# Tile 6's second product as seven half-size products, and three weight groups a stage later

## The chip, the cores and the metric

The kernel runs on one core of a Trainium2 chip. The core has a matrix engine (PE, with its weight loads shown apart as PEld), a vector engine (DVE), a scalar engine (ACT), a general engine (POOL) and a queue engine (SP) that issues DMAs here. Each engine works through its own instructions in order. [...]

The metric is the time of one execution on the device in microseconds, the median of several runs.

## What is computed

Attention with a sliding window of 64 keys over 8 batches of 8 heads, 576 positions and head size 64, and then a layer with a cosine gate over the 4608 x 512 result:

```python
scores = scale * np.matmul(q, k.transpose(0, 1, 3, 2))
rel = pos[:, None] - pos[None, :]
mask = (rel >= 0) & (rel < window)            # window = 64
attn = softmax(np.where(mask, scores, -1e9))
x = np.matmul(attn, v)                        # as (4608, 512)
h = x @ w_in                                  # (4608, 2048)
g = h * np.cos(h)
out = g @ w_out                               # (4608, 512)
```

## The kernel before

The 4608 rows are cut into nine tiles of 512 rows (mt = 0 to 8). For tiles 1 to 8 a stage has 32 units of planned time (T = 32, the first half Q = 16). In the first half PE computes h for the tile, 16 blocks of 128 columns with four matmuls each (`first`, L479). For each block ACT takes the sine (L709) and DVE multiplies (the gate, L712) into a tile gT. The h blocks go round five PSUM banks named O1, X0, X1, S and O0 (`H_BANKS`), so a bank is free for the fifth block after it once the gate has read it. In the second half PE multiplies the gates with w_out: 64 matmuls of 512 columns into banks O1 and O0, 16 per block of 128 rows, each block copied out by DVE or ACT (L723 to L727).

In tiles 7 and 8 (`FAST`) the second half is a Strassen-Winograd scheme (`fast_second`): the 512 x 2048 by 2048 x 512 product is cut into 2 x 2 blocks and done as seven products P1 to P7 of 16 matmuls of 256 columns. It needs sums of blocks of w_out (T0 to T3, `sum_weights`, L499, made over earlier stages by POOL and DVE) and sums of blocks of the gates (`sum_rows`, L511, on DVE after the last gate). The products' parts are combined when they are read from PSUM: `keep` leaves p1, t6 and t56 in SBUF, `result` writes the output. T2 and T3 lie in the buffers of q and k and are made by POOL in tile 6's stage.

Attention for the batches 2 to 7 is woven into these stages. Each batch has nine groups of four units. `burst_scores` puts the scores of several groups into PSUM at once (a first burst of four groups at 14.6 units, a second of five at 20.2). For each group follow `g_max` (mask and maximum, DVE, L347), `g_exp` (exponentials with row sums, ACT, L359), `g_inv` (reciprocal, DVE, L369), `g_norm` (POOL, L376) and `g_trans` (a transposing DMA on SP's queue, L395), one group every `PACE` = 1.44 units. `values` (L411) multiplies with v, and `put_x` copies the result, on DVE or ACT, into xT, which the next tile's h reads. Batch 7 does this in tile 6's stage; its groups 0 and 1 are needed by tile 7's values, the rest by tile 8's. Values for a tile come at the end of the stage before (T x mt - 1.01), those for tile 8 earlier (- 8.01).

The order is written out by hand: `at(time, fn, ...)` puts a step into a plan, and `pump(time)`, called after each block of h and after each piece of a product, issues everything planned up to that time. The order in which steps are issued is the order on each engine. In tile 6 before, the second half pumps one unit after every four matmuls of 512 columns; in a seven-product tile it pumps 16/14 of a unit after every eight matmuls of 256 columns.

Of the kernel before, what the change touches and what calls it, by code (L numbers as in the profile page):

```python
# [40 lines left out]
FAST = (7, 8)  # L41
PRODUCTS = ("P1", "P2", "P6", "P5", "P7", "P3", "P4")
# [27 lines left out]
def kernel(  # L70
# [45 lines left out]
    H_BANKS = [banks * 3 + [last] for *banks, last in (["O1", "X0", "X1", "S", "O0", "X0"], ["X1", "S", "X0", "O1", "O0", "S"])]  # L116
# [159 lines left out]
    for b in range(2, B):  # L276
        alone = NU // 2 if b == 3 else NU - 1
        steps = [(0, 2), (2, 4)], [(alone,)] + [(5, 7), (7, 9)] if b == 3 else [(4, 6), (6, 8), (alone,)]
        for banks, starts in zip(BURSTS, steps):
# [58 lines left out]
    def g_max(n):  # L338
# [4 lines left out]
        else:  # L343
            s = att.tile([128, GF, 128], F32, tag="s", name="s", bufs=6)
# [106 lines left out]
    def gate_half(g, f):  # L451
        if ("g", f) not in st:
            st["g", f] = moe.tile([128, 2, MT], BF16, tag="gT", name="gT", bufs=n_ff // 2 + 2)
# [22 lines left out]
    def first(mt, ff, ks, start, stop):  # L476
        if start:
            st["h", ff] = bank(H_BANKS[mt == 1][ff], "h_ps")
# [10 lines left out]

    def b_block(k_, j):  # L490
        return w_out_sb[:, n_ff // 2 * k_:n_ff // 2 * k_ + n_ff // 2, half * j:half * j + half]

    def sum_weights(i, f, engine):
        d = slice(2 * f, 2 * f + 2)
        if ("T", i) not in st:
            st["T", i] = w_sums[:, i] if i < 2 else rows_tile("qk"[i - 2])[:, 0:n_ff // 2 * half].rearrange("p (a n) -> p a n", n=half)
        in0, in1 = ((b_block(0, 1), b_block(0, 0)), (b_block(1, 1), st["T", 0]),
                    (b_block(1, 1), b_block(0, 1)), (b_block(1, 0), st.get(("T", 1))))[i]
        (nc.gpsimd if engine == "p" else nc.vector).tensor_tensor(out=st["T", i][:, d], in0=in0[:, d], in1=in1[:, d], op=ALU.subtract)  # L499

    def sum_rows(gT):
        sums = [[att.tile([128, 4, half], BF16, tag="se"[i], name="sums", bufs=6) for i in range(2)] for _ in range(4)]
        s1, s2, s3, s4 = [[pair[i // 2][:, 2 * (i % 2):2 * (i % 2) + 2] for i in range(4)] for pair in sums]
        a = [[[gT[f + 4 * k_][:, :, half * i:half * i + half] for f in range(4)] for k_ in range(2)] for i in range(2)]

        def sums_now(*which):
            for i in which:
                to, in0, in1, op = ((s1, a[1][0], a[1][1], ALU.add), (s2, s1, a[0][0], ALU.subtract),
                                    (s3, a[0][0], a[1][0], ALU.subtract), (s4, a[0][1], s2, ALU.subtract))[i]
                for f in range(4):  # L510
                    nc.vector.tensor_tensor(out=to[f], in0=in0[f], in1=in1[f], op=op)  # L511
        sums_now(0, 1)
        return sums_now, {"P1": a[0][0], "P2": a[0][1], "P4": a[1][1], "P5": s1, "P6": s2, "P7": s3, "P3": s4}

    def fast_second(mt, gT):
        sums_now, lhs = sum_rows(gT)
# [13 lines left out]
        def result(o_sb, c, of, other, block=None):  # L530
            for n in range(len(blocks)) if of == apart and block is None else (block,):
                d, lo, hi = (slice(0, 2), 0, half) if n is None else blocks[n]
                cols = slice(half * c + lo, half * c + hi)
                nc.vector.tensor_tensor(out=o_sb[:, d, cols], in0=acc[of] if n is None else acc[of][n],
                                        in1=temp[other][:, d, lo:hi], op=ALU.add)
# [7 lines left out]
        def after_p2():  # L543
            result(o1, 0, "P2", "p1")
            sums_now(2)

        def after_p6():
            keep("t6", "P6", "p1")
            sums_now(3)
# [3 lines left out]
        after = {"P1": lambda: keep("p1", "P1"), "P2": after_p2, "P6": after_p6, "P5": lambda: keep("t56", "P5", "t6"),  # L553
                 "P7": lambda: result(o2, 1, "P7", "t56"), "P3": lambda: result(o1, 1, "P3", "t56"),
                 "P4": lambda: result(o2, 0, "P7", "t6")}
        for n, name in enumerate(PRODUCTS):
# [5 lines left out]
            to = acc[name if new else "P7"]  # L562
            split = type(to) is list
            for n_, (e, lo, hi) in enumerate(blocks if split else ((0, 0, half), (1, 0, half))):
                for f in range(n_ff // 2):
                    nc.tensor.matmul(out=to[n_] if split else to[:, e], lhsT=lhs[name][f // 2][:, f % 2, 128 * e:128 * e + 128],  # L566
                                     rhs=rhs[name][:, f, lo:hi], start=new and f == 0 and (e == 0 or split),
# [22 lines left out]
    for i, (b, jobs, banks) in enumerate(bursts):  # L590
        t = T * (b - 1)
        at(t + BURST[i % 2] + 0.9 * (i == 1), burst_scores, i)
# [53 lines left out]
    for n in range(16):  # L646
# [3 lines left out]
        else:  # L650
            at(T * (FAST[0] - 1) + (5.8 if i == 2 else 9.8) + f, sum_weights, i, f, "p")
# [41 lines left out]
    for mt in range(1, n_mt):  # L693
# [5 lines left out]
        for ff in range(n_ff):  # L699
# [5 lines left out]
            if ff % 2 == 0:  # L705
                gt = moe.tile([128, 2, MT], BF16, tag="gT", name="gT", bufs=n_ff // 2 + 2)
                gT.append(gt)
            e = ff % 2
            nc.scalar.activation(sin, h_ps, AF.Sin, bias=math.pi / 2.0)  # L709
            if ff == n_ff - 1 and mt < B - 1:  # L710
                exp_table()
            nc.vector.tensor_tensor(out=gt[:, e], in0=h_ps, in1=sin, op=ALU.mult)  # L712
            pump(base + ff)
# [3 lines left out]
        for ms0 in range(0, MT // 128, 2):  # L717
            o_sb = moe.tile([128, 2, d_model], F32, tag="out", name="out_sb", bufs=OUTS)
            o_ps = [bank(which, "out_ps") for which in (("O1",) if mt == n_mt - 1 and ms0 else ("O1", "O0"))]
            for e in range(2):  # L720
                ms = ms0 + e
                for ff in range(n_ff):
                    nc.tensor.matmul(out=o_ps[e], lhsT=gT[ff // 2][:, ff % 2, ms * 128:ms * 128 + 128],  # L723
# [39 lines left out]
```

## Time and profile before

| | us |
|---|---|
| median of 3 runs | 302.15 |
| lowest, highest | 302.14, 304.46 |
| span of the profiled execution | 301.0 |
| PE busy | 294.0 (98%) |
| DVE busy | 234.7 (78%) |
| ACT busy | 232.2 (77%) |
| POOL busy | 210.3 (70%) |

The span runs from the first to the last instruction of one profiled execution. The granted PE clock is full throughout. A row of a timeline or of the chain gives the start, the length, the engine, the line of the kernel, the operation with its output and input, and a count; in brackets stands how long the engine was idle before and who released it. Busy times of PE are partly modelled, since matmuls overlap, so the distance from one start to the next says more than a row's length.

### The profile page before, as it was taken

The page shows a single profiled execution, that of the slowest core. Times are in us where ns is not written, and L with a number is a line of the kernel's source. Part 1 is how long each engine was busy: PE and PEld are TensorE (multiplying, and loading weights), DVE is VectorE, ACT ScalarE, POOL GpSimd, SP SyncE. Part 2 cuts the span into 40 slices and gives each one's busy share as a digit, 9 for nine tenths or more (in the row PEclk, how much of TensorE's full clock was granted, in tenths as well). Part 3 has the DMA queues.
Part 4 walks back from the last instruction along what each step waited for, and adds up shares of the span by engine and source line. Part 5 has one row for each costly group of instructions (what it writes and reads, how often), then busy time and mean ns, then how long its engine had stood idle before and what let it go on. Part 6 is the DMA issues. An engine that isn't in the chain of part 4 may idle for free.

```text
span 301.0 us, 8375 instructions
## 1 busy us (share of the span) xinstructions
PE 294.0 (98%) x2863; PEld 162.5 (54%) x2863; DVE 234.7 (78%) x916; ACT 232.2 (77%) x781; POOL 210.3 (70%) x238
## 2 busy tenths in 40 slices
PE   8888999999999999999999999999999999999996
PEld 3667854644455445444454445444544454785485
DVE  4997888898887886788678876887588658985794
ACT  5997699877987699769986998699978997304610
POOL 8999568995899579995999599969997860000000
PEclk9999999999999999999999999999999999999999
DMA  7999999999999994999999999999999745003013
GB/s 146 179 206 195 198 186 138 99 154 156 219 124 112 230 119 75 115 152 188 174 108 145 165 216 115 126 152 205 134 101 119 212 86 174 2 3 139 1 37 105
DMA packets 159627, 41.45 MB, mean 138 GB/s; under 512 B 146976, under 2 KB 155232, under 8 KB 159584
## 3 DMA queue, kind: packets, MB, share of 16 engines
q0 software_dynamic: 101088, 18.06, 79.6%
q1 hardware_dynamic: 58352, 22.79, 42.3%
q8 instruction: 22, 0.36, 0.5%
q14 instruction: 21, 0.17, 0.2%
q10 hardware_dynamic: 144, 0.07, 0.1%
HBM read 36.70 MB, written 9.44 MB: 153 GB/s over the span
## 4 chain that ended last, share of the span: by engine, by line
PE 90%; DMA 4%; POOL 4%; DVE 1%; issue 0%; POOLq 0%
PE h_ps L479 37%; PE out_ps L723 28%; PE out_ps L566 8%; PE out_ps L462 5%; DMA w_in<-in_moe_w_in_dram 4%; PE h_ps L443 4%; PE s_ps L310 3%; PE o_ps L411 3%; PE tq_ps L223 1%; POOL v L186 1%; POOL q L164 1%; POOL k L164 1%; PE s_ps L332 1%; POOL w_in L202 0%; DVE xT L125 0%; PE tw_ps L392 0%
## 5 line engine op out<-in xcount | busy, mean ns | idle before, releaser
L479 PE MATMUL h_ps<-xT,w_in 128*128 128x512 bf16 x512 | 115.1, 379 | 0.2
L712 DVE TENSOR_TENSOR gT<-h_ps,sin 128x512 bf16<-128x512 f32 x128 | 85.2, 688 | 25.8 <-ACT sin L709 25.2
L709 ACT ACTIVATE sin<-h_ps 128x512 f32<-128x512 f32 x128 | 73.8, 598 | 37.0 <-PE h_ps L479 36.7
L359 ACT ACTIVATE e<-s,negm 128x128 f32<-128x128 f32 (+1 forms) x256 | 97.1, 382 | 1.7 <-POOL v L125 1.0
L723 PE MATMUL out_ps<-w_out,gT 128*128 128x512 bf16 x384 | 85.3, 379 | 0.0
L376 POOL TENSOR_TENSOR w<-e,rden 128x512 bf16<-128x512 f32 (+1 forms) x68 | 69.0, 1032 | 21.8 <-DVE rden L369 15.9
L479 PEld LDWEIGHTS <-w_in 128*128 128x128 bf16 x512 | 48.9, 98 | 54.5
L723 PEld LDWEIGHTS <-gT 128*128 128x128 bf16 x384 | 36.5, 98 | 43.1
L347 DVE CUSTOM_DVE_ANT_0 s<-s_ps,mask 128x128 f32<-128x128 f32 (+1 forms) x256 | 56.0, 277 | 1.8 <-PE s_ps L332 1.5
L359 ACT ACTIVATION_READ_ACCUMULATOR e<-s,negm 128x1 f32 x256 | 48.1, 188 | 0.0
L186 POOL DMA_DIRECT2D v<-in_v_dram x40 | 34.1, 870 | 0.1
L180 POOL DMA_DIRECT2D q<-in_q_dram x36 | 28.7, 801 | 7.7 <-DMA k<-in_k_dram 3.0
L180 POOL DMA_DIRECT2D k<-in_k_dram x36 | 28.7, 799 | 1.5 <-DVE gT L712 0.7
L369 DVE RECIPROCAL rden<-den 128x4 f32<-128x4 f32 (+1 forms) x73 | 12.2, 167 | 18.7 <-ACT e L359 18.3
L125 POOL COPY v<-v 64x1536 bf16<-64x1536 bf16 (+3 forms) x16 | 22.9, 1433 | 0.4
L347 DVE DVE_READ_ACCUMULATOR2_ANT negm<- 128x1 f32 x256 | 21.3, 83 | 0.0
L125 DVE CAST xT<-o_ps 128x512 bf16<-128x512 f32 x24 | 15.6, 679 | 4.6 <-PE o_ps L411 4.4
L443 PE MATMUL h_ps<-xT,w_in 128*128 128x256 bf16 x128 | 14.6, 273 | 0.4 <-DMA w_in<-in_moe_w_in_dram 0.4
L462 PE MATMUL out_ps<-w_out,gT 128*128 128x512 bf16 x64 | 14.8, 380 | 0.0
L443 PEld LDWEIGHTS <-w_in 128*128 128x128 bf16 x128 | 12.3, 98 | 2.1 <-DMA w_in<-in_moe_w_in_dram 0.7
L566 PEld LDWEIGHTS <-sums 128*128 128x128 bf16 x136 | 12.2, 98 | 2.0 <-DVE sums L511 0.4
L449 ACT ACTIVATE sin<-h_ps 128x512 f32<-128x512 f32 x16 | 9.3, 596 | 4.2 <-PE h_ps L443 4.2
(92 smaller groups left out, 309.4 us busy)
## 6 DMA issues: line engine op xcount, KB each, us to landing
out_dram<-out_sb SPq DMA_DIRECT2D x16, 512.0 KB, 8.3
v<-in_v_dram POOLq DMA_DIRECT2D x32, 128.0 KB, 5.6
q<-in_q_dram POOLq DMA_DIRECT2D x36, 96.0 KB, 7.3
k<-in_k_dram POOLq DMA_DIRECT2D x36, 96.0 KB, 6.1
w_in<-in_moe_w_in_dram POOLq DMA_DIRECT2D x4, 512.0 KB, 9.6
w_out<-in_moe_w_out_dram POOLq DMA_DIRECT2D x4, 512.0 KB, 11.0
q<-in_q_dram POOLq DMA_DIRECT2D x7, 144.0 KB, 5.6
k<-in_k_dram POOLq DMA_DIRECT2D x7, 144.0 KB, 5.7
```

Source lines behind the costliest of these rows:

```text
L125: {"a": nc.scalar.copy, "p": nc.gpsimd.tensor_copy}.get(engine, nc.vector.tensor_copy)(out, in_)
L180: nc.gpsimd.dma_start(out=st[name, b][:, c].rearrange("p (h d) -> p h d", h=H), in_=src.rearrange("h p d -> p h d"))
L186: nc.gpsimd.dma_start(out=vt.rearrange("p (h d) -> p h d", h=H), in_=v[b, :, c * 128:c * 128 + n, :].rearrange("h p d -> p h d"))
L347: nc.vector.tensor_tensor_reduce(out=s[:, u, c], in0=s_ps[:, u, c], in1=mask[:, 2 - j % 2 if j else 0, c], scale=-scale if b else -1.0, sc ...
L359: nc.scalar.activation(e[:, u, c], s[:, u, c], AF.Exp, bias=negm[:, u:u + 1], scale=1.0 if n < n_first else -1.0, accum_out=den[:, u:u + 1])
L376: (nc.gpsimd if engine == "p" else nc.vector).tensor_tensor(out=w[:, 0:u], in0=e[:, 0:u], op=ALU.mult, in1=rden[:, 0:u].unsqueeze(2).to_br ...
L443: nc.tensor.matmul(out=h_ps[:, half * e:half * e + half], lhsT=w_in_sb[:, ks, ff * 128:ff * 128 + 128], rhs=st["xT", 0][:, ks, half * g:ha ...
L479: nc.tensor.matmul(out=st["h", ff], lhsT=w_in_sb[:, ks, ff * 128:ff * 128 + 128], rhs=st["xT", mt][:, ks], start=start, stop=stop)
L566: nc.tensor.matmul(out=to[n_] if split else to[:, e], lhsT=lhs[name][f // 2][:, f % 2, 128 * e:128 * e + 128], rhs=rhs[name][:, f, lo:hi], ...
L709: nc.scalar.activation(sin, h_ps, AF.Sin, bias=math.pi / 2.0)
L712: nc.vector.tensor_tensor(out=gt[:, e], in0=h_ps, in1=sin, op=ALU.mult)
L723: nc.tensor.matmul(out=o_ps[e], lhsT=gT[ff // 2][:, ff % 2, ms * 128:ms * 128 + 128], rhs=w_out_sb[:, ff], start=ff == 0, stop=ff == n_ff - 1)
```

## The change

`FAST` becomes (6, 7, 8). The seven products use two banks instead of three, in the order P1, P6, P2, P5, P7, P3, P4: P2 is added onto P1 in its bank after ACT has copied p1 out, P5 and then P3 onto P6 after DVE has kept t6 and t56, and P4 onto P7, which takes the bank of P1 once ACT has copied P1 + P2 to the output. The two banks swap roles from tile to tile, and `H_BANKS` of tiles 7 and 8 follow.

The halves of the inner dimension are now interleaved in pairs, four gates share one gT tile, and the first two row sums are made on DVE behind every fourth gate. The third (a difference) overwrites gate blocks in place: in tile 6 on DVE after P6, in tiles 7 and 8 on POOL behind every fourth gate. The fourth is made on DVE after P2. The buffers of s go from six to four.

Batch 7's second burst has two groups left; its last three groups get a burst of their own in tile 7's stage at 14.6 units, and tile 8's values move to the usual place. ACT loads the table of the exponential in tile 7 as well.

```diff
-FAST = (7, 8)
-PRODUCTS = ("P1", "P2", "P6", "P5", "P7", "P3", "P4")
+FAST = (6, 7, 8)
+LATE = 6
+FAMILY = ("O1", "O0")
+PRODUCTS = ("P1", "P6", "P2", "P5", "P7", "P3", "P4")
...
+    H_BANKS = {mt: ["X0", "X1", FAMILY[(mt - FAST[0]) % 2], "S", FAMILY[(mt - FAST[0] + 1) % 2]] * 3 + ["X0"] for mt in FAST[1:]}
+    H_BANKS[1] = ["X1", "S", "X0", "O1", "O0"] * 3 + ["S"]
+    H_BANKS.update({mt: ["O1", "X0", "X1", "S", "O0"] * 3 + ["X0"] for mt in range(2, FAST[0] + 1)})
...
+        if b == B - 1:
+            cut = (BURSTS[0], steps[0]), (("S", "X0"), steps[1][:1]), (("t", "t", "t"), steps[1][1:])
...
-            s = att.tile([128, GF, 128], F32, tag="s", name="s", bufs=6)
+            s = att.tile([128, GF, 128], F32, tag="s", name="s", bufs=4)
...
+    w_out_b = w_out_sb.rearrange("p (g k e) n -> p k g e n", k=2, e=2)
...
+    def sum_rows(mt, gT, g, which, engine=None):
...
+        for i in which:
+            to, in0, in1, op = ((s1, a[1][0], a[1][1], ALU.add), (s2, s1, a[0][0], ALU.subtract),
+                                (a[1][0], a[0][0], a[1][0], ALU.subtract), (s2, a[0][1], s2, ALU.subtract))[i]
+            (nc.gpsimd if engine == "p" else nc.vector).tensor_tensor(out=to, in0=in0, in1=in1, op=op)
...
-        at_bank = {"P1": "O1", "P2": "O0", "P6": "X1", "P5": "O1", "P7": "O0", "P3": "X1"}
+        one, two = FAMILY if (mt - FAST[0]) % 2 == 0 else FAMILY[::-1]
+        at_bank = {"P1": one, "P6": two, "P7": one}
+        onto = {"P2": "P1", "P5": "P6", "P3": "P6", "P4": "P7"}
...
+                if other is None:
+                    copy("a", o_sb[:, d, cols], acc_)
...
         def after_p6():
             keep("t6", "P6", "p1")
-            sums_now(3)
+            if mt == FAST[0]:
+                for g in groups_:
+                    sum_rows(mt, gT, g, (2,))
+
+        def after_p2():
+            result(o1, 0, "P1", None)
+            for g in groups_:
+                sum_rows(mt, gT, g, (3,))
...
+        late = i == len(bursts) - 1
+        at(t + T + 14.6 if late else t + BURST[i % 2] + 0.9 * (i == 1), burst_scores, i)
...
+            if late:
+                time = t + T + 15.2 + PACE * (place - LATE)
+                for lag, fn in zip((0.2, 1.5, 3, 3.2, 3.8), (g_max, g_exp, g_inv, g_norm, g_trans)):
+                    at(time + lag, fn, n)
+                continue
...
-            time = T * mt - (8.01 if mt == n_mt - 1 else 1.01)
+            time = T * mt - 1.01
...
-            at(T * (FAST[0] - 1) + (5.8 if i == 2 else 9.8) + f, sum_weights, i, f, "p")
+            at(T * FAST[0] + (5.8 if i == 2 else 9.8) + f, sum_weights, i, f, "p")
...
-            if ff == n_ff - 1 and mt < B - 1:
+            if ff == n_ff - 1 and mt < B:
                 exp_table()
             nc.vector.tensor_tensor(out=gt[:, e], in0=h_ps, in1=sin, op=ALU.mult)
+            if mt in FAST and e == 3:
+                sum_rows(mt, gT, ff // 4, (0, 1))
+                if mt > FAST[0]:
+                    sum_rows(mt, gT, ff // 4, (2,), "p")
```

More of the change, by code (lines that the diff above doesn't have):

```diff
@@ L278 @@
         steps = [(0, 2), (2, 4)], [(alone,)] + [(5, 7), (7, 9)] if b == 3 else [(4, 6), (6, 8), (alone,)]
-        for banks, starts in zip(BURSTS, steps):
+        cut = zip(BURSTS, steps)
+        if b == B - 1:
+            cut = (BURSTS[0], steps[0]), (("S", "X0"), steps[1][:1]), (("t", "t", "t"), steps[1][1:])
+        for banks, starts in cut:
             jobs = []
@@ L477, in first @@
         if start:
-            st["h", ff] = bank(H_BANKS[mt == 1][ff], "h_ps")
+            st["h", ff] = bank(H_BANKS[mt][ff], "h_ps")
         nc.tensor.matmul(out=st["h", ff], lhsT=w_in_sb[:, ks, ff * 128:ff * 128 + 128],
@@ L722 @@
                 for ff in range(n_ff):
-                    nc.tensor.matmul(out=o_ps[e], lhsT=gT[ff // 2][:, ff % 2, ms * 128:ms * 128 + 128],
+                    nc.tensor.matmul(out=o_ps[e], lhsT=gT[ff // 4][:, ff % 4, ms * 128:ms * 128 + 128],
                                      rhs=w_out_sb[:, ff], start=ff == 0, stop=ff == n_ff - 1)
```

60 lines of the change are left out of this document (28 added, 32 removed).

## The prediction

> **What bounds the kernel now.** I read the page's first part, then the chain that ended last in order of time for the last three tiles, then the timeline of each engine there.
>
> ```profile
> span 301.0 us, 8375 instructions
> PE 294.0 (98%) x2863; PEld 162.5 (54%) x2863; DVE 234.7 (78%) x916; ACT 232.2 (77%) x781; POOL 210.3 (70%) x238
> ```
>
> ```profile
> 213.83 13.97 PE h_ps L479 x64
> 227.80 0.52 PE s_ps L310 x32
> 228.33 5.29 PE out_ps L723 x24
> 233.61 0.79 PE s_ps L310 x40
> 234.41 8.74 PE out_ps L723 x40
> 243.15 0.43 PE o_ps L411 x16
> ...
> 244.34 13.97 PE h_ps L479 x64
> 258.31 7.11 PE out_ps L566 x64
> 265.42 1.13 PE o_ps L411 x64
> 266.55 5.35 PE out_ps L566 x48
> 271.90 13.81 PE h_ps L479 x64
> 285.71 12.40 PE out_ps L566 x128
> ```
>
> The columns are start, length, engine and line. PE is busy for 98% of the span and its pieces follow each other with hardly a gap, so only what shortens or stalls PE counts. Tile 6 runs from 213.83 to 244.34 (30.51 us), tile 7 to 271.90 (27.56), tile 8 to the end. A full-size product takes 8.74 / 40 = 0.2185 us per matmul, so 64 take 13.98; in tile 7 (already seven products) 112 matmuls take 7.11 + 5.35 = 12.46, 0.111 each, 1.78 per product. Tiles 7 and 8 show no stall that could be regained.
>
> **What the change can win.** Only tile 6 has a product left to shorten: 13.98 - 12.46 = 1.52 us. The three groups' 24 score matmuls move from tile 6 to tile 7 (0.79 / 40 x 24 = 0.47 each way) and cancel. Everything before 213.83 keeps its order and its banks; four buffers for s instead of six delay nothing, since each reciprocal of group n already stands ahead of the maxima of group n+4 in DVE's queue. Gates four to a tile, and the new grouping of w_out, change addresses only, and each bank that a product or a next tile's h takes was read a product earlier. So the ceiling is 0.5% and the question is what stalls are bought.
>
> **Prices on DVE**, start to start:
>
> ```profile
> 216.81 3.71 DVE L712 TENSOR_TENSOR gT<-h_ps,sin 128x512 bf16<-128x512 f32 x6 [1.78 <-ACT sin L709]
> ...
> 239.70 0.29 DVE L347 CUSTOM_DVE_ANT_0 s<-s_ps,mask 128x128 f32<-128x128 f32 x1
> ...
> 240.55 0.69 DVE L125 COPY out_sb<-out_ps 128x512 f32<-128x512 f32 x1
> 241.15 0.17 DVE L369 RECIPROCAL rden<-den 128x4 f32<-128x4 f32 x1
> ...
> 243.60 1.29 DVE L125 CAST xT<-o_ps 128x512 bf16<-128x512 f32 x2 [0.79 <-PE o_ps L411]
> ```
>
> ```profile
> 259.59 1.42 DVE L511 TENSOR_TENSOR sums<-gT 128x512 bf16<-128x512 bf16 x4
> ```
>
> A gate takes (3.71 - 0.69) / 5 = 0.604 (0.69 is the full length of an operation on a whole bank), a group's maxima 240.55 - 239.70 = 0.85, an operation on a whole bank 241.15 - 240.55 = 0.60, a row sum (1.42 - 0.42) / 3 = 0.335, with 0.42 its full length by the rows' mean.
>
> **ACT in tile 6.** By the times in the plan and the new steps of the pump (16/14 of a unit per half product, each 0.89 us on PE), ACT's order behind the last sine is: table, exponentials of group 0, copy of P1, groups 1, 2, 3, copy of P1+P2, groups 4, 5.
>
> ```profile
> 228.46 1.28 ACT L471 ACT_TABLE_LOAD   x1
> ...
> 229.86 0.33 ACT L359 ACTIVATE e<-s,negm 128x64 f32<-128x64 f32 x1
> ...
> 235.80 0.39 ACT L359 ACTIVATE e<-s,negm 128x128 f32<-128x128 f32 x1
> ...
> 237.34 0.57 ACT L125 COPY out_sb<-out_ps 128x512 f32<-128x512 f32 x1
> 237.81 0.40 ACT L359 ACTIVATE e<-s,negm 128x128 f32<-128x128 f32 x1
> ```
>
> Groups 0 to 3 take 235.80 - 229.86 = 5.94 without a gap, group 4 takes 1.54 (so groups 0 and 1, half of them 64 wide, (5.94 - 3.08) / 2 = 1.43 each), a copy 0.47 (0.57 to its end). Group 0's maxima come two row sums later (0.67), so ACT starts at about 230.1. P1's copy ends at 230.1 + 1.43 + 0.57 = 232.1; P2, which adds into P1's bank, could start at 228.33 + 3.56 = 231.89 and waits 0.3. The copy of P1+P2 stands behind group 3: 230.1 + 5.94 + 0.47 = 236.5, some 0.3 more because group 3's maxima wait on DVE for t6 and four differences, end 237.3. P7, in the same bank, could start at 228.33 + 4 x 1.78 + 0.32 (16 score matmuls) = 235.8. PE so stands at 237.3 rather than 235.8: 1.5 of the 1.52 is gone at P7, and even with ACT never waiting on DVE 1.1 would be.
>
> **DVE in tile 6.** In the second half DVE must do six groups (5.1), reciprocals (0.17 each, with zeroing 1), eight row sums (2.7), the last two of the first half (0.67) and four bank operations (2.4): 11.9 us in a window of 12.46 + 0.32 = 12.8. After P5, t56 waits in that queue behind the differences for P3 and group 5's maxima and ends at about 239.5; P3 adds into the bank it reads and could start at 237.3 + 1.78 = 239.1: 0.5. With P2's wait (already inside the 1.5) the second product ends at about 243.2, where it ends now (243.15): the gain is gone. At the seam DVE's result of P4 (0.60) now stands ahead of the first xT cast, so the next tile's first matmul follows 0.60 + (1.29 - 0.60) + 0.1 for two hand-overs = 1.4 us behind the product instead of 244.34 - 243.15 = 1.19: +0.2.
>
> **Tile 7.** ACT: copy of P1, groups 6 to 8 (4.6), copy of P1+P2. From the end of the first half: P1's copy at 0.48 + 1.78 = 2.3, groups 2.8 to 7.4, copy to 8.0; P7 could start at 0.48 + 4 x 1.78 = 7.6. P5 waits 0.4 for t6, which DVE holds behind group 6's reciprocal and group 8's maxima, so the two overlap: 0.45 together. The values, now in the middle with their casts hidden, move behind P4 with the casts exposed: the seam above is 1.38 for 1.13 + 0.03, +0.25 on top of scores 0.47. Together 0.45 + 0.25 + 0.47 = +1.2, of which 0.47 is tile 6's. The tables (1.28 each way) lie in ACT's idle time. Tile 8's first half waits for casts as tile 6's does: 13.97 for 13.81, +0.16. What of it lies on POOL and SP:
>
> ```profile
> 218.98 1.15 POOL L499 TENSOR_TENSOR q<-w_out 128x512 bf16<-128x512 bf16 x1
> ...
> 223.09 1.17 POOL L499 TENSOR_TENSOR k<-w_out,w_sums 128x512 bf16<-128x512 bf16 x1
> ...
> 227.18 1.18 POOL L499 TENSOR_TENSOR k<-w_out,w_sums 128x512 bf16<-128x512 bf16 x1
> ...
> 231.68 1.04 POOL L376 TENSOR_TENSOR w<-e,rden 128x512 bf16<-128x512 f32 x1 [1.50 <-DVE rden L369]
> ```
>
> ```profile
> 235.90 14.01 SPq L395 DMA_TRANSPOSE wT<-w  x9
> ```
>
> ```profile
> wT<-w SPq DMA_TRANSPOSE x12, 2.5
> ```
>
> POOL's four differences in each of tiles 7 and 8 (1.17 as its weight sums) run beside gates, and the last, behind row sums that end at about 2, is done at 3.2 for P7 at 7.6 (tile 8: 7.1). SP's nine transposes in tile 6 (14.01 / 9 = 1.56 each) become six; the late three follow POOL's products. Group 8's exponentials end at 7.4, reciprocal and product (1.04) at 8.9, the transpose lands 2.5 later, at 11.4; the values come at 0.48 + 12.46 + 0.45 = 13.4, so 2 us cover it. SP's stores of tile 6 stand before them and wait for nothing by then. The spread of v and groups 4 and 5 on POOL are needed in tile 8 alone.
>
> Queues alone: tile 6 +0.2, tile 7 +1.0 net of what tile 6 gives it, tile 8 +0.16: +1.4.
>
> **The row sums against POOL in tile 6.** Eight of them stand among the gates, and POOL is then busy with the weight sums (the rows from 218.98, 223.09 and 227.18 above, with a DMA issue behind each).
>
> ```profile
> 56.89 2.30 POOL L180 DMA_DIRECT2D k<-in_k_dram  x3
> ...
> 83.81 1.04 POOL L125 COPY v<-v 64x1024 bf16<-64x1024 bf16 x1
> ```
>
> ```profile
> 57.77 0.68 DVE L376 TENSOR_TENSOR w<-e,rden 128x512 bf16<-128x512 f32 x1
> ...
> 83.94 1.46 DVE L376 TENSOR_TENSOR w<-e,rden 128x512 bf16<-128x512 f32 x1
> ```
>
> The same DVE operation with both inputs in SBUF took 0.68 beside POOL's DMA issues and 1.46 when a POOL copy had started 0.13 before it: it stood still until that copy (83.81 + 1.04) was nearly over. Gates have an input in PSUM and are not held. Row sums have both in SBUF.
>
> [...]
>
> Row sum 0 comes at 216.81 + 4 x 0.604 = 219.2 and waits for the one from 218.98: 0.85. With 0.67 of its own the gates are 1.5 late and catch up 0.26 each (PE gives one per 13.81 / 16 = 0.863). The next comes at about 223.1, a toss against the one from 223.09: held 1.0, gate 8 starts at 224.8 and frees its bank at 225.5, which PE wants at 213.83 + 52 x 0.216 = 225.06: 0.5 of stall. The third comes at about 227.2, again a toss against 227.18: held, gate 12 ends at 229.6 and with it bank X1, into which the scores of 227.80 go; P1 starts 1.9 late, group 0's maxima another 0.4: 2.3 to 2.5 in all. [...] Ends: 0 (no such block for bf16) and 2.5; I take 1.3, since every order that I worked out with the 1.46 row gives at least 1.2. The differences for P3 meet a product of POOL once more: 0.2.
>
> Sum: 1.4 + 1.3 + 0.2 = +2.9. The profiled execution's span is 301.0 and the median of the runs 302.15, 1.1 above; I keep that distance: span 304.0, median 305.0, 1.0% slower, on the edge of what a measurement of this kernel can tell from no change (about 1%).
>
> **Rivals.** *The port holds three groups* (slower): tosses two and three go to POOL, +1.4 + 2.5 + 0.2 = +4.1, 306.2. It decides when gate 12 ends after 228.3. For it: 223.09 and 227.18 lie 0.1 before DVE. *Queues alone*: the bf16 sums aren't held; +1.4, 303.5. Against it the 1.46. *The gain comes through* (not slower): the copy of P1+P2 isn't late because ACT gets to it before 235.8; 1.52 less the seams (0.2 + 0.25 + 0.16) and part of tile 7's 0.45 is -0.5 to -0.9, about 301.4. Against it: 5.94 of exponentials stand ahead of that copy. *Waits by whole tile*: writing a quarter of a gate tile in place holds every reader of that tile; P1 in tiles 7 and 8 would wait 2 us for POOL's last difference, P2 in tile 6 about 2.5 for DVE's four: +1.4 + 6.5, 310. Against it: PE began tile 7 at 244.34 while the second cast of 243.60, into the same xT tile, was still writing.
>
> **How the numbers follow.** Forecast (mild order of the port, 304.2 to 305.6) 0.40; three groups held (305.7 to 306.8) 0.27; queues alone (302.6 to 304.2) 0.18; gain through (300.6 to 302.5) 0.10; whole tile 0.05. Range 301.8 to 306.8: left out are the whole-tile case and most of the gain's lower half, and tails, under 2 in 10. Slower by over 1% (above 305.17): 0.27 + 0.05 + 0.05 of the forecast's upper end = 0.37; faster by over 1% (below 299.1) is beyond the ceiling: 0.01; within 1%: 0.62.
>
> **What would show it.** ACT's copy of P1+P2 in tile 6 behind four groups of exponentials, and PE idle about 1.4 at P7 and 0.5 at P3 with ACT and DVE as releasers; row sums among tile 6's gates of 0.8 to 1.5 us instead of 0.42, while those of tiles 7 and 8 are 0.42; first scores of tile 6 late behind gate 12; PE idle 0.4 in tile 7 and an xT cast behind the result of P4 at both seams. I am wrong if P7 starts as P5 ends in tile 6, or if no row sum exceeds 0.5 us.

## The result, and the profile after

| | before | after |
|---|---|---|
| median of 6 runs each, us | 302.45 | 311.5 |
| lowest, highest | 302.14, 304.46 | 311.33, 312.55 |
| span of the profiled execution | 301.0 | 309.7 |

The ratio is 1.0286, with a 95% interval of 1.0251 to 1.032: the changed kernel is slower. The forecast was 305.0 with a range to 306.8. The sign was right and the size was not.

The page of the profiled execution after (first part, then the first line of the chain that ended last):

```profile
span 309.7 us, 8500 instructions
PE 294.7 (95%) x2911; PEld 167.4 (54%) x2911; DVE 242.5 (78%) x925; ACT 236.0 (76%) x786; POOL 220.7 (71%) x246
...
PE 72%; DVE 17%; DMA 5%; POOL 2%; ACT 2%; issue 1%; POOLq 0%; ACTq 0%; DVEq 0%
```

PE is as busy as it was (294.7 against 294.0), so nearly all of the 8.7 us is PE standing still, and DVE now holds 17% of the chain (1% before). The timeline of PE after shows where (start, length, what; in brackets the idle time before the row and who ended it):

```profile
213.67 7.93 PE L488 MATMUL h_ps<-xT,w_in 128*128 128x512 bf16 x36
223.38 3.61 PE L488 MATMUL h_ps<-xT,w_in 128*128 128x512 bf16 x16 [1.78 <-DVE gT L740]
227.54 2.82 PE L488 MATMUL h_ps<-xT,w_in 128*128 128x512 bf16 x12 [0.55 <-DVE gT L740]
231.39 0.59 PE L317 MATMUL s_ps<-kT,qT 64*64 64x64 bf16 x32 [1.03 <-DVE gT L740]
231.91 1.92 PE L588 MATMUL out_ps<-w_out,gT 128*128 128x256 bf16 x16
...
236.34 1.03 PE L588 MATMUL out_ps<-w_out,gT 128*128 128x256 bf16 x8 [0.77 <-ACT p L129]
...
241.52 1.91 PE L588 MATMUL out_ps<-q,gT 128*128 128x256 bf16 x16 [1.06 <-DVE s L524]
243.95 1.91 PE L588 MATMUL out_ps<-w_out,s 128*128 128x256 bf16 x16 [0.52 <-DVE t L544]
...
247.53 1.20 PE L418 MATMUL o_ps<-wT,v 128*64 128x64 bf16 x64
248.98 4.48 PE L488 MATMUL h_ps<-xT,w_in 128*128 128x512 bf16 x20 [0.25 <-DVE xT L129]
254.05 9.66 PE L488 MATMUL h_ps<-xT,w_in 128*128 128x512 bf16 x44 [0.59 <-DVE gT L740]
...
284.05 9.66 PE L488 MATMUL h_ps<-xT,w_in 128*128 128x512 bf16 x44 [0.59 <-DVE gT L740]
```

Among the h of tile 6 PE waits three times for gates, 1.78 + 0.55 + 1.03 = 3.36 us. In its second product P2, P7 and P3 wait, 2.35 together. Tiles 7 and 8 each lose 0.59 in the same place, at the sixth h.

Everything below is counted from tile 6's first h to the end of the span, because the part before it, in which all kernels of the table do the same, varies by 1.5 us from one profiled execution to another. The columns are the distances between starts of PE's rows on the timeline: tile 6's first h, the first matmul of its second product (P1 where there are seven), tile 7's first h, tile 8's first h, and the end of the span. Before the change two of these starts are

```profile
228.26 5.35 PE L723 MATMUL out_ps<-w_out,gT 128*128 128x512 bf16 x24
...
271.74 13.98 PE L479 MATMUL h_ps<-xT,w_in 128*128 128x512 bf16 x64
```

The prediction took 27.56 for tile 7 from the chain, where a row begins only when the one before has ended; by the timeline's starts it is 27.40.

| us | tile 6, h | tile 6, product and seam | tile 7 | tile 8 | sum |
|---|---|---|---|---|---|
| before | 14.43 | 16.08 | 27.40 | 29.3 | 87.2 |
| after | 18.24 | 17.07 | 30.00 | 30.7 | 96.0 |
| table ahead | 18.25 | 17.08 | 28.94 | 29.4 | 93.7 |
| no weight sums on POOL | 14.74 | 16.52 | 30.00 | 30.7 | 91.9 |
| both | 14.84 | 16.43 | 28.94 | 29.4 | 89.6 |
| no late groups | 18.27 | 17.75 | 27.45 | 29.3 | 92.8 |
| tile 6 plain, table ahead | 14.43 | 15.64 | 28.94 | 29.4 | 88.4 |
| both, queues ordered | 14.43 | 16.08 | 29.64 | 29.4 | 89.5 |

Why the gates are late is read on DVE and POOL. Row sums among tile 6's gates, after:

```profile
219.17 1.07 DVE L524 TENSOR_TENSOR s<-gT 128x512 bf16<-128x512 bf16 x1
220.27 2.46 DVE L524 TENSOR_TENSOR s<-s,gT 128x512 bf16<-128x512 bf16 x1
...
225.15 1.27 DVE L524 TENSOR_TENSOR s<-gT 128x512 bf16<-128x512 bf16 x1
226.46 0.43 DVE L524 TENSOR_TENSOR s<-s,gT 128x512 bf16<-128x512 bf16 x1
...
229.31 0.96 DVE L524 TENSOR_TENSOR s<-gT 128x512 bf16<-128x512 bf16 x1
```

POOL beside them:

```profile
216.57 3.38 POOL L510 TENSOR_TENSOR q<-w_out 128x512 bf16<-128x512 bf16 x3
219.90 0.94 POOL L190 DMA_DIRECT2D v<-in_v_dram  x1
220.86 1.17 POOL L510 TENSOR_TENSOR q<-w_out 128x512 bf16<-128x512 bf16 x1
221.97 0.93 POOL L190 DMA_DIRECT2D v<-in_v_dram  x1
```

A row sum beside no weight sum takes 0.43 (226.46). The first one was held until the third weight sum was over (216.57 + 3.38 = 219.95), the second until after the fourth (220.86 + 1.17 = 222.03; it ended at 222.73). The four long ones are over by 1.07 + 2.46 + 1.27 + 0.96 - 4 x 0.42 = 4.08.

In tiles 7 and 8 the row sums are short. There it is ACT, on its timeline after:

```profile
248.52 0.58 ACT L129 CAST xT<-o_ps 128x512 bf16<-128x512 f32 x1 [4.06 <-PE o_ps L418]
251.38 1.28 ACT L737 ACT_TABLE_LOAD   x1 [2.27 <-PE h_ps L488]
252.67 2.56 ACT L737 ACTIVATE sin<-h_ps 128x512 f32<-128x512 f32 x5
```

By the profile the load of the sine table stands idle for 2.27 us, in tile 8 as in tile 7, until PE has finished the first h, and only then takes its 1.28. Before the change it ran right behind the cast, with no idle time in front, and in tile 8 there was none:

```profile
245.04 1.28 ACT L709 ACT_TABLE_LOAD   x1
```

The sine at 252.67 starts as the load ends (251.38 + 1.28 = 252.66), with no wait of its own. That the load stands there with the first sine's wait for PE's h is the author's reading of these rows.

### The profile page after: what moved, and what is told of

Read it like the earlier page. It is cut to its first block, busy times and chain, and to the rows that moved or that the text cites. A ratio compares the mean times of both kernels' runs of the same rounds, so it can differ in the third digit from the quotient of the medians.

```text
span 309.7 us, 8500 instructions
## 1 busy us (share of the span) xinstructions
PE 294.7 (95%) x2911; PEld 167.4 (54%) x2911; DVE 242.5 (78%) x925; ACT 236.0 (76%) x786; POOL 220.7 (71%) x246
## 4 chain that ended last, share of the span: by engine, by line
PE 72%; DVE 17%; DMA 5%; POOL 2%; ACT 2%; issue 1%; POOLq 0%; ACTq 0%; DVEq 0%
PE h_ps L488 26%; PE out_ps L755 23%; DVE gT L740 9%; PE out_ps L588 7%; PE out_ps L471 5%; DVE s L524 5%; PE h_ps L450 4%; DMA w_in<-in_moe_w_in_dram 3%; PE s_ps L317 2%; PE o_ps L418 2%; DMA q<-in_q_dram 2%; PE tq_ps L227 1%; DVE s L354 1%; POOL v L190 1%; ACT e L366 1%
## 5 line engine op out<-in xcount | busy, mean ns | idle before, releaser
L740 DVE TENSOR_TENSOR gT<-h_ps,sin 128x512 bf16<-128x512 f32 x128 | 83.0, 685 | 23.2 <-ACT sin L737 22.5
L737 ACT ACTIVATE sin<-h_ps 128x512 f32<-128x512 f32 x128 | 73.4, 599 | 31.4 <-PE h_ps L488 27.7
L488 PEld LDWEIGHTS <-w_in 128*128 128x128 bf16 x512 | 48.9, 98 | 59.2 <-issue 5.3
L755 PE MATMUL out_ps<-w_out,gT 128*128 128x512 bf16 x320 | 71.1, 379 | 0.0
L755 PEld LDWEIGHTS <-gT 128*128 128x128 bf16 x320 | 30.4, 98 | 35.9
L524 POOL TENSOR_TENSOR gT<-gT 128x512 bf16<-128x512 bf16 x8 | 10.6, 1329 | 31.8 <-DVE s L524 31.8
L184 POOL DMA_DIRECT2D k<-in_k_dram x36 | 28.8, 804 | 1.4 <-DVE gT L740 0.8
L588 PEld LDWEIGHTS <-gT 128*128 128x128 bf16 x208 | 18.8, 98 | 5.2 <-issue 1.5
L588 PEld LDWEIGHTS <-s 128*128 128x128 bf16 x144 | 13.9, 98 | 3.7 <-issue 1.5
L129 ACT CAST xT<-o_ps 128x512 bf16<-128x512 f32 x12 | 7.1, 593 | 11.2 <-PE o_ps L418 11.2
L450 PE MATMUL h_ps<-xT,w_in 128*128 128x256 bf16 x128 | 14.6, 273 | 0.2 <-DMA w_in<-in_moe_w_in_dram 0.2
```

What stands on the lines that cost most here:

```text
L129: {"a": nc.scalar.copy, "p": nc.gpsimd.tensor_copy}.get(engine, nc.vector.tensor_copy)(out, in_)
L184: nc.gpsimd.dma_start(out=st[name, b][:, c].rearrange("p (h d) -> p h d", h=H), in_=src.rearrange("h p d -> p h d"))
L450: nc.tensor.matmul(out=h_ps[:, half * e:half * e + half], lhsT=w_in_sb[:, ks, ff * 128:ff * 128 + 128], rhs=st["xT", 0][:, ks, half * g:ha ...
L488: nc.tensor.matmul(out=st["h", ff], lhsT=w_in_sb[:, ks, ff * 128:ff * 128 + 128], rhs=st["xT", mt][:, ks], start=start, stop=stop)
L755: nc.tensor.matmul(out=o_ps[e], lhsT=gT[ff // 4][:, ff % 4, ms * 128:ms * 128 + 128], rhs=w_out_sb[:, ff], start=ff == 0, stop=ff == n_ff - 1)
```

## The experiments

Three theories. *Port*: POOL's weight sums hold the row sums of tile 6 (the 3.8 us of its h stage). *Table*: the late sine table makes the gates of tiles 7 and 8 late. *Queues*: the places of exponentials, maxima and copies in ACT's and DVE's order cost the rest. The rival to port and table was that row sums among the gates are too much for DVE by themselves. Each ratio below is against the kernel before, run again beside it; its median there lay between 303.43 and 303.77.

### The sine table ahead

```diff
             skewed(mt, ks, ks)
+        if mt > FAST[0]:
+            sine_table()
         for ff in range(n_ff):
```

> The changed kernel with one more small sine (128x1) on ScalarE at the end of the first projection's opening pairs in tiles 7 and 8, so that the sine table is loaded there and not in front of the first real sine, where the load waits for the first h (251.38 and 281.38 after). Theory 'table': the load runs right behind the xT cast, the first gate of both tiles comes 1.2 to 1.3 us earlier, TensorE's idle times of 0.59 us at the fifth h of each tile go, and with them 0.28 and 0.15 later in tile 8: the span falls by 1.2 to 2.0 us from 309.7, to 307.7 to 308.5. Rival 'queue': the row sums on VectorE, not the load, make the gates late; the idle times come back at the next row sums, and the span falls by less than 0.5 us. Tile 6 keeps its 35.3 us under both.

Measured: 309.54 us, ratio 1.02 (1.0159 to 1.024). ACT and, below it, PE in tile 7 of this run:

```profile
250.32 1.28 ACT L483 ACT_TABLE_LOAD   x1
```

```profile
250.18 13.97 PE L488 MATMUL h_ps<-xT,w_in 128*128 128x512 bf16 x64 [0.25 <-DVE xT L129]
```

The load follows the cast, and the 64 matmuls of h run through in 13.97 as in tile 7 before. The time from tile 6's first h to the end falls by 2.36, from 96.0 to 93.7, all of it in tiles 7 and 8. That is a little more than forecast: P5's wait in tile 7 falls from 0.65 to 0.44 as well. The span fell by only 1.2 because the part ahead of tile 6 came out 1.2 longer here. *Table* holds. Its rival falls: row sums behind every four gates do not delay PE when nothing else does.

### POOL's weight sums left out

```diff
-        rhs = {"P1": b_block(0, 0), "P2": b_block(1, 0), "P4": st["T", 3], "P5": st["T", 0], "P6": st["T", 1],
-               "P7": st["T", 2], "P3": b_block(1, 1)}
+        rhs = {"P1": b_block(0, 0), "P2": b_block(1, 0), "P4": b_block(1, 0), "P5": st["T", 0], "P6": st["T", 1],
+               "P7": b_block(1, 1), "P3": b_block(1, 1)}
...
-        else:
-            at(T * FAST[0] + (5.8 if i == 2 else 9.8) + f, sum_weights, i, f, "p")
```

> The changed kernel without POOL's eight subtractions of output weights in tile 6 (the last two of the four weight sums; the products P7 and P4 take a plain block of the weights instead, so those quarters of three tiles are not the reference's). Theory 'port': VectorE's row sums in tile 6 are held up by these eight and by nothing else; each takes 0.42 to 0.46 as in tiles 7 and 8, tile 6's stage of h goes from 18.24 us back to 14.0 to 15.0, and the span falls by 3.2 to 4.2 us, to 305.5 to 306.5. Rival 'issue': POOL's DMA issues between the subtractions (0.9 us each) hold VectorE as well; row sums of over 1 us stay beside them and the span falls by 1 to 2.5. Rival 'queue': the row sums are in the gates' way at any length; the stage stays above 16 and the span falls by less than 1.5.

Measured: 307.87 us, ratio 1.0155 (1.0103 to 1.0207). DVE and then POOL in tile 6:

```profile
217.10 2.48 DVE L738 TENSOR_TENSOR gT<-h_ps,sin 128x512 bf16<-128x512 f32 x4 [1.78 <-ACT sin L735]
219.62 0.42 DVE L524 TENSOR_TENSOR s<-gT 128x512 bf16<-128x512 bf16 x1
220.08 0.42 DVE L524 TENSOR_TENSOR s<-s,gT 128x512 bf16<-128x512 bf16 x1
220.43 2.48 DVE L738 TENSOR_TENSOR gT<-h_ps,sin 128x512 bf16<-128x512 f32 x4
```

```profile
217.02 4.27 POOL L190 DMA_DIRECT2D v<-in_v_dram  x5
```

The h stage falls from 18.24 to 14.74 and the sum by 4.07 (96.02 to 91.95). *Port* holds with its full size. The first two row sums lie beside POOL's five DMA issues and take 0.42: here issuing alone held nothing, and the rival *issue* falls. One more thing is read here: four gates and a pair of row sums take 220.43 - 217.10 = 3.33 of DVE while PE needs 13.81 / 4 = 3.45 for four h. A delay once taken is recovered by 0.12 per four gates, so hardly at all.

### Both together

> The table ahead and no weight sums on POOL in tile 6, both together (the same two blocks of the products left plain). If 'port' and 'table' are separate causes the two gains add: a span lower by 4.4 to 6.2 us than 309.7, 303.5 to 305.3, so still 2.5 to 4.3 over the kernel before: what is left is the queues of ScalarE and VectorE in the second products and the late groups. If both only shorten the same queue of VectorE, the sum falls short of the two by over 1 us.

Measured: 305.46 us, ratio 1.0072 (1.0034 to 1.0109). The sum is 89.6, and 96.0 - 89.6 = 6.4 is the two gains added, 4.07 + 2.36. The two causes are separate. 2.35 us over the kernel before are left: tile 6's product and seam 0.35, its h 0.4, tile 7 1.5, tile 8 0.05. The 0.4 of h lies in the scores, half of it a wait of 0.21 for a transposed q; in the run with both and the queues ordered, at the end of this section, nothing delays them and the stage takes 14.43 as before.

### No late groups

```diff
-        if b == B - 1:
-            cut = (BURSTS[0], steps[0]), (("S", "X0"), steps[1][:1]), (("t", "t", "t"), steps[1][1:])
...
-        late = i == len(bursts) - 1
+        late = False
...
-            time = T * mt - 1.01
+            time = T * mt - (8.01 if mt == n_mt - 1 else 1.01)
...
-            if ff == n_ff - 1 and mt < B:
+            if ff == n_ff - 1 and mt < B - 1:
```

> The changed kernel with the last three weight groups of batch 7 back in tile 6 (five groups in the second burst as in the other batches, the values of tile 8 again seven units earlier, no exp table in tile 7). Theory 'late groups cost tiles 7 and 8': tile 7 loses its scores (0.48), the wait of P5 (0.65) and the dearer seam (0.25) and tile 8 its table load, so the two fall from 30.00 + 30.72 to 28.2 to 28.8 + 29.0 to 29.8, that is by 2.1 to 3.5 us; tile 6 gains three groups of exps, maxima and norms in the two-bank product, and grows by 2 to 4 us from 35.31. The span changes by -1 to +1.5. Rival 'tile 6 has room': tile 6 grows by less than 1 us and the span falls by 1.5 to 3.

Measured: 308.72 us, ratio 1.0193 (1.0129 to 1.0256). Tiles 7 and 8 fall to 27.45 and 29.3, as they were before, and tile 6 grows by only 0.7: its product still had room for three more groups, and the rival came true (span 307.0). In this run tile 8 needs no sine table, and tile 7's load runs at 250.33 without waiting for the first h (250.19). So the late groups bring the late tables with them. Beside the run with the table ahead, the late groups themselves cost tiles 7 and 8 1.5 us and save tile 6 the 0.7.

### Tile 6 plain

`FAST` is (7, 8) with the new order, banks and late groups kept in tiles 7 and 8, and the table ahead.

> The changed kernel with the table ahead, but tile 6's second product plain as before (no row sums in its gates; weight sums on POOL in tile 6 as in both kernels): tiles 7 and 8 alone have the two banks and the row sums behind every four gates, and the three late groups stay late. Tile 6 without its three last groups: 29.6 to 30.5 us from its first h to the next (before 30.5); tiles 7 and 8 as with the table ahead, 28.9 and 29.4. From tile 6's first h to the end 88.0 to 88.9 us, 0.8 to 1.7 over before: what the new order in tiles 7 and 8 and the late groups cost by themselves. If the row sums in the gates of tiles 7 and 8 cost nothing and the late groups nothing, it is 87.2 or less.

Measured: 304.3 us, ratio 1.0022 (1.0001 to 1.0043), the sum 88.4. Once the table is ahead, tiles 7 and 8 take 1.6 us more than before, and tile 6, which has three groups less, 0.4 less: 1.15 us together. The other 93.7 - 88.4 = 5.3 us of the run with the table ahead hang on the product of tile 6.

### The weight sums moved

The next question was whether the sums can be made elsewhere, with the table ahead and nothing left out. First on DVE in tile 5's second product:

```diff
-            at(T * FAST[0] + (5.8 if i == 2 else 9.8) + f, sum_weights, i, f, "p")
+            late_sums = (23.35, 24.78, 28.4, 28.5) if i == 2 else (20.47, 21.91, 24.79, 27.67)
+            at(T * (FAST[0] - 1) + late_sums[f], sum_weights, i, f, "v")
```

> The changed kernel with the table ahead, and with the last two of the four weight sums moved off POOL and out of tile 6: VectorE makes them in the second product of tile 5, beside the waits that it has there for ScalarE. Nothing is left out. Theory 'port': what held the row sums was POOL's subtraction itself, so moving it is worth as much as leaving it out: the stage of h of tile 6 at 14.5 to 15.0 us, from tile 6's first h to the end 89.3 to 90.3 us (after 96.0), the span 303.4 to 304.6. Rival: the eight subtractions cost VectorE and ScalarE in tile 5 what they saved: tile 5 grows by 1.5 to 3 us, and the span stays above 305.

Measured: 312.34 us, ratio 1.0297 (1.0255 to 1.0339). The rival came true, by holds like those that *port* names. DVE, POOL and PE of this run:

```profile
209.35 2.11 DVE L510 TENSOR_TENSOR k<-w_out,w_sums 128x512 bf16<-128x512 bf16 x1
```

```profile
207.48 3.69 POOL L129 COPY v<-v 64x1536 bf16<-64x1536 bf16 x2
```

```profile
218.09 15.42 PE L488 MATMUL h_ps<-xT,w_in 128*128 128x512 bf16 x64 [3.48 <-DVE xT L129]
```

A subtraction of 0.42 was held 2.11 by a copy of v, others by POOL's norms (1.29 from 213.79, 2.35 for two from 215.09), DVE fell behind, and PE waited 3.48 for the casts at the head of tile 6.

Then split, between the gates of tile 5 and behind POOL's norms at the head of tile 6, with the two sums' buffers exchanged:

```diff
-            to = w_sums[:, i] if i < 2 else rows_tile("qk"[i - 2])[:, 0:n_ff // 2 * half].rearrange("p (a n) -> p a n", n=half)
+            to = w_sums[:, i] if i < 2 else rows_tile("kq"[i - 2])[:, 0:n_ff // 2 * half].rearrange("p (a n) -> p a n", n=half)
...
-            at(T * FAST[0] + (5.8 if i == 2 else 9.8) + f, sum_weights, i, f, "p")
+            at(T * (FAST[0] - 1) + (9.5 + f if i == 2 else 24.79 if f == 3 else T + 5.8 + f / 100), sum_weights, i, f, "v" if i == 2 or f == 3 else "p")
```

> The changed kernel with the table ahead and nothing left out; the last two weight sums are put where VectorE and POOL do not both compute from SBUF: the third (four subtractions) on VectorE between the gates of tile 5, where POOL only issues loads; of the fourth one on VectorE in tile 5's second product and three on POOL right behind the norms at the head of tile 6, ahead of the first row sum. Theory 'port': the row sums of tile 6 take 0.42 to 0.46 (the first at most 1), tile 6's stage of h is 14.5 to 15.3 us and the time from its first h to the end 89.3 to 90.5, as with the sums left out; tile 5 grows by 0.3 at most; the span 303.3 to 305. Rival 'VectorE has no room': tile 5's gates fall behind and TensorE waits there for 1 us or more.

Measured: 312.92 us, ratio 1.0312 (1.0278 to 1.0346). Tile 6's row sums took 0.42 and 0.43 as expected, and from tile 6's first h to the end the run takes 90.3, inside the expected 89.3 to 90.5: *port* holds in a kernel that leaves nothing out. But tile 5 lost more than that won (tile 6's first h comes at 220.82 for 213.67), and DVE's timeline there shows why:

```profile
200.65 0.42 DVE L510 TENSOR_TENSOR k<-w_out 128x512 bf16<-128x512 bf16 x1 [6.01 <-DMA k<-in_k_dram]
```

The buffer of k was not free yet (by the profile a load into k had not landed): DVE stood 6.01 us in front of this write, and the gates of tile 5 with it (PE idle 4.82).

### The queues

On top of the sums made early: in tile 6 the exponentials of the first group go behind ACT's copy of P1 and those of the fourth behind its copy of P1+P2, maxima behind t56; in tile 7 the last group's maxima and the first reciprocal go behind t6.

> As the run with the sums early, and with groups of the last batch at other places in the queues: in tile 6 the exps of the first group behind ScalarE's copy of P1, those of the fourth behind its copy of P1+P2, the maxima of the sixth behind VectorE's sum t56; in tile 7 the maxima of the last group and the first reciprocal behind t6. Theory 'queues': the waits of P2 (0.2), P7 (1.0) and P3 (0.6) in tile 6 and of P5 (0.4) in tile 7 go, and the time from tile 6's first h to the end falls by 1.5 to 2.2 us, to 87.3 to 88.4, against 87.2 before the change. Rival 'VectorE full': the waits move to the next sum of VectorE, and less than 0.8 us is won.

Measured: 317.51 us, ratio 1.0457 (1.0432 to 1.0482). P2, P7 and P3 were to gain; P2 and P7 wait for nothing now, and P3 waits 5.46. DVE's and POOL's rows:

```profile
243.09 5.38 DVE L524 TENSOR_TENSOR s<-gT,s 128x512 bf16<-128x512 bf16 x4
```

```profile
242.35 2.21 POOL L383 TENSOR_TENSOR w<-e,rden 128x512 bf16<-128x512 f32 x2 [1.91 <-DVE rden L376]
244.52 3.69 POOL L129 COPY v<-v 64x1536 bf16<-64x1536 bf16 x2
```

The four row sums for P3, 1.42 when alone, now lie beside two norms and the copies of v and end with them (244.52 + 3.69 = 248.21). In the changed kernel they were over before those copies began. With the values of tile 8 four units earlier on top:

> As the run with the order changed, and the values of tile 8 four units earlier, among the last products of tile 7, so that their casts are not behind the result of P4. Expected: the seam from tile 7's P4 to the first h of tile 8 loses its idle 0.25 us and some of the 1.45, 0.2 to 0.6 us in all; the span 300.5 to 302.5, level with the kernel before. If the weights of the last three groups are not there in time, TensorE waits for them and the run is slower than the one with the order changed.

Measured: 320.67 us, ratio 1.0559 (1.0535 to 1.0584): PE stands 2.70 us in the middle of P3 of tile 7, for the values, whose weights had not landed (by the profile the DMA into wT).

The split sums with the same order, and POOL's copies of v behind the fourth group's norm (its product with the reciprocals):

> As the run with the sums split, with the queue places of the run with the order changed (exps behind ScalarE's two copies, maxima and reciprocals behind t6 and t56), and POOL's two copies of v in tile 6 put behind the norm of the fourth group, so that they no longer meet the four last row sums. Theory 'queues and port': P2, P7 and P5 wait for nothing, the last row sums take 1.4 to 2.2 instead of 5.38, P3 waits at most 0.6; from tile 6's first h to the end 87.3 to 88.6 us (before 87.2), the span 301.2 to 302.8. If the copies of v are then late for the values of tile 7, TensorE waits at the seam behind tile 6 for 0.5 to 2 us.

Measured: 313.99 us, ratio 1.0362 (1.0322 to 1.0402), the sum 89.7; the loss is tile 5's. The four row sums took 2.43 beside norms instead of 5.38, P2 and P7 of tile 6 and P5 of tile 7 waited for nothing, P3 of tile 6 2.50, more than expected: t56 stood behind the row sums and the fifth group's maxima.

The same with the values of tile 8 two units earlier:

> As the run before it, with the values of tile 8 two units earlier, inside the last product of tile 7. If the weights of the last three groups are there, the seam ahead of tile 8 loses 0.2 to 0.5 us, and the span is 300.8 to 302.6, level with the kernel before. If they are not, TensorE waits for them and it is 0.3 to 1 us slower than the run before it.

Measured: 315.57 us, ratio 1.0385 (1.0349 to 1.042). Tile 7 takes 29.9 for 28.8: PE waits 1.79 for the values, so the weights are not there two units earlier either.

Last, the run with both (weight sums left out as above) and every place in the queues that had mattered:

> The run with both (table ahead, POOL's eight subtractions of weights left out of tile 6, so that P7 and P4 use plain blocks), and with every queue place that the traces so far have shown to matter: ScalarE's two copies ahead of the exps, the last row sums and t56 ahead of the fifth and sixth groups' maxima, POOL's copies of v behind the fourth group's norm, t6 of tile 7 ahead of maxima and reciprocal. It asks what the change could give at best, with the price of the weight sums taken as nothing. Theory 'queues': P2, P7 and P5 wait for nothing, P3 for at most 0.5 us, and from tile 6's first h to the end it is 86.8 to 88.0 us, level with the 87.2 before the change, in time within 0.7% of the kernel before. Rival 'the idea gains when its queues are clear': 85.7 or less, over 0.5% faster than before. Rival 'VectorE full': P3 still waits 1 us or more, and it is over 88.5.

Measured: 305.19 us, ratio 1.0055 (1.0029 to 1.0081). PE of this run:

```profile
229.56 1.92 PE L588 MATMUL out_ps<-w_out,gT 128*128 128x256 bf16 x16
...
237.04 1.91 PE L588 MATMUL out_ps<-w_out,gT 128*128 128x256 bf16 x16
240.60 1.91 PE L588 MATMUL out_ps<-w_out,s 128*128 128x256 bf16 x16 [1.66 <-DVE t L544]
...
244.19 1.20 PE L418 MATMUL o_ps<-wT,v 128*64 128x64 bf16 x64
...
274.28 0.98 PE L418 MATMUL o_ps<-wT,v 128*64 128x64 bf16 x50 [1.42 <-DMA wT<-w]
```

By numbers it is the rival *VectorE full*, 89.5. P3 still waits 1.66 for t56, again behind row sums held beside two norms (2.43 from 237.52); and the last three groups, now later, reach tile 8's values 1.42 late. The product of tile 6 without that wait is 244.19 - 229.56 - 1.66 = 12.97: the seven half-size products do what they should. Without both waits the sum would be about 86.4, some 0.8 us under the kernel before, for a kernel that makes no weight sums for P7 and P4. No run beat the kernel before. None of them points to one that would, though that is argued and not shown: the sums have to be made somewhere, and each place tried cost more than 0.8.

## Why the prediction was wrong

The sum was 1.4 + 1.3 + 0.2 = 2.9; tile 6 to the end grew by 8.8. The runs divide that into 4.07 (port), 2.36 (table) and 2.35 (the rest, where the forecast had 1.4 and 0.2).

- *The row sums against POOL in tile 6*: the hold was there (left out, the weight sums gave back 4.07), and the size was the largest miss, 4.07 for 1.3, outside the ends of 0 and 2.5. The 1.3 supposed that DVE would come first once and shift POOL's weight sums by 0.3; no run shows that. After the change they start at 222.91, 224.95 and 226.99, as far apart as before (223.09, 225.13, 227.18), and DVE was held in all three groups. Two more steps failed. "Row sum 0 ... waits for the one from 218.98: 0.85" counted one hold per group; in the first group both row sums were held, 0.65 and 2.04 longer than 0.42. The fourth weight sum, behind which the second one ended, stands at 221.04 in the kernel before, and is not among the rows that the prediction quoted. And the gates were to "catch up 0.26 each", with 0.67 for a pair of row sums. A pair takes 220.43 - 219.62 = 0.81, because each row sum started only when DVE's operation before it was over (219.62 behind 217.10 + 2.48 = 219.58, 220.08 behind 219.62 + 0.42 = 220.04), so that four gates and a pair recover only 0.12. So 4.08 of holds lengthened the stage by 3.8. The lower end was excluded rightly by the 1.46 row; the upper end was not an end.
- *"The tables (1.28 each way) lie in ACT's idle time"*: this failed outright, 2.36 us where the sum had nothing. There is idle time enough, but the load did not run in it: it stood 2.27 us until PE had finished the first h. No row was quoted for that step, and none asked what the load itself waits for.
- *Tile 7, +1.2*: with the table ahead it is 28.94 for 27.40, +1.5, by the steps named: scores, P5's wait (0.44) for t6, the casts behind the result of P4 (seam 1.45 for a forecast 1.4). Right in kind, some 0.3 short. The sum took 1.0 instead of 1.2, as net of tile 6; but tile 6's product, put at an end of 243.2, was already without the moved scores, so there was nothing to take off, and its own terms give 1.5 rather than 1.4.
- *Tile 8, +0.16*: 0.05 to 0.08 with the table ahead. Its h take 13.81 from start to start, as before, so the step that was named isn't seen; it was small either way.
- *ACT and DVE in tile 6*: P2's and P7's waits were put at 1.5 together; they were 1.83, and 1.19 with the weight sums left out. The copy of P1+P2 did stand behind four groups of exponentials: moved ahead of the fourth, P7 waited for nothing. The profile puts P7's wait down to a row sum for P3, but P7 does not read that: the first of the four row sums below ended at 241.38, ACT's copy below at 241.37, and in the run with both and the queues ordered P7 starts at 237.04, ahead of the first such row sum at 237.52. P3's 0.5 was 0.52. Right, and *the gain comes through* falls with it. With product and seam at 16.52 for 16.08, the +0.2 was 0.2 short.

```profile
240.62 1.76 DVE L524 TENSOR_TENSOR s<-gT,s 128x512 bf16<-128x512 bf16 x4
```

```profile
240.81 0.56 ACT L129 COPY out_sb<-out_ps 128x512 f32<-128x512 f32 x1
```

- *The differences for P3 meet a product of POOL: 0.2*: 1.76 - 1.42 = 0.34 in tile 6, small only because of where it fell; the run with the order changed shows 5.38 - 1.42 = 4.0 for the same four operations.
- *The ceiling of 1.52*: the seven products without P3's wait take 12.97, for 12.46 and 0.32 of scores forecast. Right within 0.2.
- *Waits by whole tile*: no product waited for a POOL operation on another quarter; that rival was rightly small.
- The 1.1 between span and median became 1.8, which adds 0.7 to the median. In every run on record an execution takes 1.7 to 1.9 longer than its own span, so the 1.1 came from setting a median against the span of another execution.

So the range failed because its upper end was made of the "toss" for one hold, and the table loads had no term at all. Neither of the two signs of being wrong came (P7 did wait, and four row sums among the gates took over 0.5); there was none for a time above the range.

## What to carry to other kernels

A short vector operation with both inputs in SBUF had no fixed price here: 0.42 beside nothing or beside POOL's DMA issues, 0.96 to 2.46 beside its weight sums, 2.11 beside a copy. Place such operations by what POOL computes there, and check the place again after every reordering. When a delay is priced, ask how much slack per round the engine has to recover it; at 0.12 per 3.45 a hold is paid almost in full. A table load has a place in the queue and can stand there: 2.27 us here in front of a sine that needed PE's h, and none behind the cast with a small sine at 250.32. Put it where it is to run by a small operation that waits for nothing late.

## What the runs showed of the hardware

The second row sum of tile 6 took 2.46 from 220.27, though by the profile POOL then issued a DMA and computed only from 220.86; in the run without weight sums the same row sum beside an issue took 0.42. That an operation of 1.17 holds another for over two is not explained by any run here, and the profile's spans on POOL are rough. It stays open. The gates, with one input in PSUM, were not held: four took 2.48 from 216.65, beside the weight sums of 216.57, as four took 2.48 in the run without weight sums.

PE lost speed behind long waits. In the run with the order changed, PE's rows behind two waits, and the windows from there (stretch, width, busy times of PE, PEld, DVE, ACT and POOL, granted clock, DMA share, GB/s):

```profile
217.87 16.81 PE L488 MATMUL h_ps<-xT,w_in 128*128 128x512 bf16 x64 [3.47 <-DVE xT L129]
...
249.98 3.57 PE L588 MATMUL out_ps<-w_out,s 128*128 128x256 bf16 x16 [5.46 <-DVE t L544]
```

```profile
217.87:234.61 16.74, 16.74 (x64) 6.87 (x64) 12.41 (x23) 8.74 (x15) 5.25 (x6) 0.83 1.05 118
249.98:255.69 5.71, 5.71 (x33) 4.11 (x33) 2.31 (x13) 1.99 (x11) 3.07 (x3) 0.62 0.26 48
```

Behind an idle 3.47 us the 64 matmuls of h took 16.81 instead of 13.97 at a mean granted clock of 0.83, and behind 5.46 the clock was 0.62. Waits of 1.78 in the changed kernel (granted clock 1.00 over the 16 matmuls behind it) and 2.50 in the run with the split sums and the order changed cost nothing of the kind (the products after the 2.50 took 1.91 each as ever). A wait of 2.70 was not free: in the run with the values of tile 8 four units earlier, P4 of tile 7, which followed it by 3.15 us, took 3.37 for 1.91. So a long wait cost up to 2.8 us more than its length. How much more varied: with the sums made early, 3.48 us of idle cost 15.42 - 13.97 = 1.45, at a mean granted clock of 0.90 from 218.09 to 233.44, where it was 0.83 here behind 3.47. From what length on a wait costs speed, and how long PE must be busy until it has it back, these runs do not show.
